# Windowed attention with sink tokens, then a highway layer: a reordered loop, sinks' scores by the batch, and the last batch's loads in runs

## The chip, the cores and the metric

One core of a Trainium2 chip runs the kernel. The metric is the device time of one execution in microseconds; the time of a kernel is the median of its runs. Five engines have queues of their own and work in the order in which their instructions were issued: TensorE (PE, with its weight loads listed as PEld), VectorE (DVE), ScalarE (ACT), GpSimd (POOL) and SyncE (SP, here for DMAs alone). They wait for one another through semaphores.

## The reference

Two layers. The first is attention of 4 batches, 8 heads, 768 tokens and 64 dimensions, in which a token sees itself and the 127 before it, and the first 4 tokens (the sinks). The second mixes each of the 3072 tokens' 512 values with a gated function of itself.

```python
keep = is_sink | in_window                      # pos < 4, or 0 <= rel < 128
scores = np.where(keep, scale * q @ k.T, -1e9)
x = softmax(scores) @ v                         # (B, H, S, D) -> (B*S, H*D)
H = np.maximum(x @ w_h, 0.0)
T = 1.0 / (1.0 + np.exp(-(x @ w_t + b_t)))
out = T * H + (1.0 - T) * x                     # = x + T * (H - x)
```

## The kernel before

The tokens are cut into 24 tiles of 128, six to a batch (`NC`), numbered n = 0 to 23; `b, t = divmod(n, NC)`. Each tile goes through these steps:

- `scores(n)`: TensorE multiplies the keys of tile n with the queries of tiles n and n+1, 16 products of 32 rows, four heads' groups on four row groups. The last tile of a batch has only its own queries.
- `expo(n)`: ScalarE takes the exponential of all of it into E.
- `mask(n)`: VectorE multiplies E by a mask of zeros and ones (the window).
- `sink_scores(n)`, `sink_expo(n)`: for t >= 2, whose windows do not reach the sinks, the scores of the sinks' keys (`sk`, 32 columns used, padded to 128) and their exponential into `es`.
- `values(n)`: TensorE multiplies E of tiles n-1 and n with V, 16 products; for t >= 2 two more with the sinks' values `vs` against `es`. V has a column of ones, so the sum of the weights comes out beside the values.
- `norm(n)`: VectorE takes the reciprocal of the sums and multiplies: X.
- `x_transpose(n)`, `x_copy(n)`: TensorE transposes X into PSUM, ScalarE copies it to XT.
- `bias(n)`, `gate(n)`, `tanh(n)`: TensorE adds the bias (a product with a row of ones) and x @ w_t; ScalarE takes tanh of half of it. `gate_on_act(n)` on ScalarE or, for n = 16 to 22, `gate_value(n)` on GpSimd turns that into T = (tanh + 1) / 2.
- `hidden(n)`: TensorE, x @ w_h. `diff(n)`: VectorE, max(H, 0) - X. `gated(n)`: VectorE, times T, the product of the text.
- `finish(n)`: GpSimd adds X, and SP stores the tile.

The order on every engine is the order in which the program issues (`_keep_traced_order`, L19). After a start written out by hand (L466 to L551), a loop runs from s = 2 to 21 (L552 to L599). A pass is named here by n2 = s + 2, the tile whose scores it computes, 4 to 23; it also handles n1 = s + 1 (mask, values, norm), n0 = s (transpose, gate, hidden) and n9 = s - 1 (difference, product, output). In a pass VectorE's order is diff(n9), mask(n1), gated(n9), transposes of loaded data, then the reciprocal and X of n1. TensorE's is sink_scores(n2), x_transpose(n0), scores(n2), bias(n0), half of gate(n0), values(n1), the other half, hidden(n0). ScalarE's is sink_expo, x_copy, expo, tanh, T. After the loop comes an end written out by hand (L601 to L638).

Queries and keys come from memory with a cast to 16 bits through GpSimd's queue (`load_part`, `load_whole`), 32 partitions at a time, and VectorE transposes them in blocks of 32 (`transpose_qk`, L129; `transpose_tile`, L137). Of batches 0 to 2 a partition gets runs of 8 or 12 neighbouring tokens, and the transposes write with that step; `nat` holds them. Of batch 3 (`whole`) a partition gets single tokens, 32 apart, and the transposes, one for each of six tiles from pass 16 to 21, write neighbouring words. The table `pieces` says in which pass the transposes are, the table `loads` in which pass, and on which side of the output, the loads are issued. `sink_keys(b)` and `sink_values(b)` make `sk` and `vs` by masks. A matmul's result lies in one of the PSUM tiles ps_s (scores), ps_v (values, and in its second half the transposed X), ps_z (gate, and the sinks' scores before it) and ps_h (hidden).

Of the kernel before, what the change touches and what calls it, by code (L numbers as in the profile page):

```python
# [10 lines left out]
FP16 = mybir.dt.float16  # L11
# [21 lines left out]
def kernel(  # L33
# [27 lines left out]
    G = 4  # L61
# [45 lines left out]
    def load_part(b, i, g, which, into=None, engine=pool):  # L107

        t0, nt = segments[b][which][i]
        into = nat[b][which][i] if into is None else into  # L110
        engine.dma_start(  # L111
            out=into[32 * g:32 * g + 32].rearrange("p hg m d -> p hg (m d)"),
            in_=(q, k)[which][b, :, t0:t0 + nt, :].rearrange(
                "(g hg) (r m) d -> g r hg (m d)", g=G, m=nt // 32)[g])

    def load_whole(g, which):
        pool.dma_start(
            out=whole[32 * g:32 * g + 32, which].rearrange("p hg m d -> p (hg m) d"),
            in_=(q, k)[which][B - 1].rearrange(
                "(g hg) (m r) d -> g r (hg m) d", g=G, r=32)[g])  # L120

    def part_loads(b, i, which):

        return [lambda g=g: load_part(b, i, g, which) for g in range(G)]
# [12 lines left out]
    def transpose_tile(n):  # L137

        b, t = divmod(n, NC)
        dst = tr[b].bitcast(FP32).rearrange("p w hg t e -> p (w hg) (t e)")  # L140
        src = whole.bitcast(FP32).rearrange("p w hg m d -> p (w hg) (m d)")
        dve.transpose(out=dst[:, :, t * P:(t + 1) * P], in_=src[:, :, t * P:(t + 1) * P])
# [6 lines left out]
    def load_v_heads(b, h0, h1):  # L149
        pool.dma_start(  # L150
            out=vt[b][0][:, h0:h1].rearrange("p h t e -> p (h t) e")[:, :, 0:D],
            in_=v[b, h0:h1].rearrange("h (t p) d -> p (h t) d", p=P))
# [8 lines left out]
    wt = const.tile([P, KC, DM], FP16, tag="wt")  # L161
    brow = const.tile([P, DM], FP16, tag="brow")
    b32 = const.tile([1, DM], FP32, tag="b32")
    ones = const.tile([P, P], FP16, tag="ones")
    zeros = const.tile([P, H * (D + 1)], FP16, tag="zeros")
    vs32 = const.tile([H * NSINK, B, D + 1], FP32, tag="vs32")
    vmask = const.tile([H * NSINK, H], FP32, tag="vmask")
    skmask = const.tile([P, HG, H], FP16, tag="skmask")
    vs = [const.tile([P, H, D + 1], FP16, tag=f"vs{b}", name=f"vs{b}") for b in range(B)]

    sk = [const.tile([P, HG, 2, P], FP16, tag=f"sk{b}", name=f"sk{b}") for b in range(B)]
# [8 lines left out]
    sp.dma_start(out=b32, in_=moe_b_t.unsqueeze(0))  # L180
    for b in range(B):
        sp.dma_start(out=vs32[:, b, 0:D],
                     in_=v[b, :, 0:NSINK, :])
# [14 lines left out]
    dve.memset(brow, 0.0)  # L198
    dve.memset(skmask, 0.0)
    for g in range(G):  # L200
        for hg in range(HG):
            h = HG * g + hg
            dve.memset(skmask[32 * g:32 * g + 32, hg, h:h + 1], 1.0)
    for tile_v in [tile_v for of_batch in vt for tile_v in of_batch]:
        dve.memset(tile_v[:, :, :, D:D + 1], 1.0)
    dve.memset(vs32[:, :, D:D + 1], 1.0)
    for i in range(2):
        dve.memset(es[i], 0.0)
    dve.memset(sk[0].rearrange("p hg e x -> p (hg e x)"), 0.0)
    dve.memset(vs[0].rearrange("p h e -> p (h e)"), 0.0)  # L210
    for b in range(1, B):
        act.copy(out=vs[b].rearrange("p h e -> p (h e)"), in_=zeros)
        act.copy(out=sk[b].rearrange("p hg e x -> p (hg e x)"), in_=zeros[:, 0:HG * 2 * P])
# [7 lines left out]
    pool.memset(vmask, 1.0)  # L221
    pool.affine_select(out=vmask, in_=vmask, compare_op=ALU.is_ge, fill=0.0, base=0,
                       pattern=[[-NSINK, H]], channel_multiplier=1)
    pool.affine_select(out=vmask, in_=vmask, compare_op=ALU.is_ge, fill=0.0,
                       base=NSINK - 1, pattern=[[NSINK, H]], channel_multiplier=-1)


    def sink_keys(b, engine=pool):
        for hg in range(HG):
            engine.tensor_tensor(  # L230
                out=sk[b][:, hg, :, 0:H * NSINK].rearrange("p e (h s) -> p e h s", s=NSINK),
# [5 lines left out]
    def sink_values(b):  # L237
        pool.tensor_tensor(
            out=vs[b][0:H * NSINK],
            in0=vs32[:, b].unsqueeze(1).to_broadcast([H * NSINK, H, D + 1]),  # L240
            in1=vmask.unsqueeze(2).to_broadcast([H * NSINK, H, D + 1]), op=ALU.mult)
# [12 lines left out]


    def sink_bank(n):
        return (ps_h if n == 3 else ps_z)[:, 0:P]

    def sink_scores(n):
        b, t = divmod(n, NC)  # L260
        first = True
        for hg in range(HG):
            for e in range(2):
                last = hg == HG - 1 and e == 1
                pe.matmul(sink_bank(n),
                          lhsT=sk[b][:, hg, e],
                          rhs=tr[b][:, 0, hg, t * P:(t + 1) * P, e], start=first, stop=last)
                first = False

    def sink_expo(n):  # L270
        nrow = H * NSINK
        act.activation(out=es[n % 2][0:nrow], in_=sink_bank(n)[0:nrow],
                       func=AF.Exp, bias=ebias[0:nrow], scale=SCALE)
# [24 lines left out]

    def values(n):
        b, t = divmod(n, NC)  # L300
        both = av_of(n)
        for i in range(2):
            if t >= 2:
                pe.matmul(both[:, i], lhsT=es[n % 2],
                          rhs=vs[b][:, HB * i:HB * i + HB, :].rearrange("p h e -> p (h e)"),
                          start=True, stop=False, skip_group_check=True)
# [14 lines left out]
    def norm(n):  # L321
# [3 lines left out]
        dve.reciprocal(out=rec, in_=av[:, :, :, D])  # L325
# [348 lines left out]
```

## Time and profile before

| | |
|---|---|
| median of 3 runs | 120.01 us (119.53 to 120.34) |
| the profiled execution | 119.51 us, its span 117.5 us |
| granted clock of TensorE, mean | 0.987 |
| TensorE's first instruction after the loop (bias of tile 22) | starts at 106.70 us |
| DMA | 17.52 MB in 46,160 packets, 38,594 of them under 512 B |

The span is what the profile shows, from the first instruction to the last; the profiled execution took 2.0 us more than that. A line of a group gives the program line, engine, operation, the tiles and shapes, the count, the busy time and the mean in ns, and the idle time before it with its releaser. A line in order of time starts with the start and the duration in us; a bracket shows an idle stretch before it. A window's line has its bounds, its length, then the busy time of PE, PEld, DVE, ACT and POOL with the number of instructions, TensorE's clock, the share of the DMA engines and GB/s.

### The profile page before, as it was taken

The page shows a single profiled execution, that of the slowest core. Times are in us where ns is not written, and L with a number is a line of the kernel's source. Part 1 is how long each engine was busy: PE and PEld are TensorE (multiplying, and loading weights), DVE is VectorE, ACT ScalarE, POOL GpSimd, SP SyncE. Part 2 cuts the span into 40 slices and gives each one's busy share as a digit, 9 for nine tenths or more (in the row PEclk, how much of TensorE's full clock was granted, in tenths as well). Part 3 has the DMA queues.
Part 4 walks back from the last instruction along what each step waited for, and adds up shares of the span by engine and source line. Part 5 has one row for each costly group of instructions (what it writes and reads, how often), then busy time and mean ns, then how long its engine had stood idle before and what let it go on. Part 6 is the DMA issues. An engine that isn't in the chain of part 4 may idle for free.

```text
span 117.5 us, 3064 instructions
## 1 busy us (share of the span) xinstructions
PE 101.4 (86%) x1189; PEld 55.8 (48%) x1189; DVE 97.1 (83%) x186; ACT 91.0 (77%) x116; POOL 85.7 (73%) x118
## 2 busy tenths in 40 slices
PE   5997868599969869799999898999998999999920
PEld 1333445345535435556554454655464556555610
DVE  5589875669995899999998999698889998797580
ACT  0985789659769969899699999798788987964510
POOL 6979997499998997798979999530674336415660
PEclk9999999999999999999999999999999999999995
DMA  3999999989999999999999999999310222022032
GB/s 102 238 204 149 140 144 199 147 116 154 106 153 153 284 280 249 182 169 187 206 213 150 198 164 200 154 196 207 108 72 17 89 95 86 3 95 89 27 150 91
DMA packets 46160, 17.52 MB, mean 149 GB/s; under 512 B 38594, under 2 KB 42434, under 8 KB 46147
## 3 DMA queue, kind: packets, MB, share of 16 engines
q0 software_dynamic: 41744, 9.97, 96.9%
q1 hardware_dynamic: 3938, 6.72, 16.8%
q10 hardware_dynamic: 464, 0.66, 2.2%
q8 instruction: 9, 0.15, 0.5%
q14 instruction: 5, 0.03, 0.1%
HBM read 21.01 MB, written 6.29 MB: 232 GB/s over the span
## 4 chain that ended last, share of the span: by engine, by line
PE 38%; DMA 22%; DVE 21%; issue 8%; POOL 4%; ACT 3%; ACTq 1%; DVEq 0%
PE ps_z L365 10%; DMA wh<-in_moe_w_h_dram 9%; PE ps_h L398 9%; DMA nat<-in_k_dram 5%; DVE DD L402 5%; DMA first<-in_q_dram 5%; DVE E L289 5%; DVE tr L134 4%; PE ps_v L316 4%; PE ps_s L250 3%; DVE X L326 3%; DMA nat<-in_q_dram 3%; PE ps_v L313 2%; DVE DD L406 2%; PE ps_v L353 2%
## 5 line engine op out<-in xcount | busy, mean ns | idle before, releaser
L281 ACT ACTIVATE E<-ps_s,ebias 128x2048 f16<-128x2048 f32 (+1 forms) x24 | 43.7, 1822 | 2.1 <-PE ps_s L250 2.1
L411 POOL TENSOR_TENSOR O<-DD,X 128x512 f32<-128x512 f16 (+1 forms) x24 | 27.1, 1134 | 21.4 <-DVE DD L406 13.1
L365 PE MATMUL ps_z<-wt,XT 128*128 128x512 f16 (+1 forms) x96 | 27.6, 375 | 0.4
L398 PE MATMUL ps_h<-wh,XT 128*128 128x512 f16 (+1 forms) x96 | 24.2, 374 | 1.4 <-DMA wh<-in_moe_w_h_dram 1.4
L289 DVE TENSOR_TENSOR E<-E,mask_std 128x2048 f16<-128x2048 f16 (+1 forms) x20 | 22.8, 1138 | 0.3 <-ACT E L281 0.2
L134 DVE STREAM_TRANSPOSE tr<-nat 128x512 f32<-128x512 f32 (+1 forms) x22 | 19.0, 909 | 2.1 <-DMA nat<-in_q_dram 1.1
L402 DVE SCALAR_TENSOR_TENSOR DD<-ps_h,X 128x512 f16<-128x512 f32 (+1 forms) x24 | 16.2, 677 | 4.3 <-PE ps_h L398 3.5
L382 ACT ACTIVATE TH<-ps_z 128x512 f16<-128x512 f32 (+1 forms) x24 | 14.1, 586 | 5.3 <-PE ps_z L365 4.9
L358 ACT COPY XT<-ps_v 128x512 f16<-128x512 f16 x23 | 13.1, 571 | 5.5 <-PE ps_v L353 5.4
L316 PE MATMUL ps_v<-v,E 128*128 128x65 f16 x184 | 15.4, 195 | 1.8 <-DVE E L289 1.5
L326 DVE TENSOR_TENSOR X<-ps_v,rec 128x512 f16<-128x512 f32 x23 | 15.9, 692 | 0.9
L250 PE MATMUL ps_s<-tr 32*128 32x256 f16 (+1 forms) x384 | 14.3, 264 | 1.5 <-DVE mask L492 0.9
L398 PEld LDWEIGHTS <-XT 128*128 128x128 f16 x100 | 9.7, 98 | 11.8 <-issue 1.5
L316 PEld LDWEIGHTS <-E 128*128 128x128 f16 x192 | 12.2, 97 | 6.4 <-DVE E L289 5.1
L313 PE MATMUL ps_v<-v,E 128*128 128x65 f16 x152 | 15.0, 193 | 0.1
L111 POOL DMA_DIRECT2D nat<-in_k_dram x24 | 13.4, 571 | 0.6 <-DMA nat<-in_k_dram 0.6
L313 PEld LDWEIGHTS <-E 128*128 128x128 f16 x160 | 12.5, 98 | 2.3 <-issue 0.2
L111 POOL DMA_DIRECT2D nat<-in_q_dram x20 | 11.2, 564 | 2.2 <-DMA wh<-in_moe_w_h_dram 1.5
L353 PE MATMUL ps_v<-ident,X 128*128 128x128 f16 x92 | 9.0, 220 | 4.2 <-DVE X L326 4.0
L388 ACT ACTIVATE TH<-TH,half 128x512 f16<-128x512 f16 (+1 forms) x17 | 12.0, 709 | 0.5
L191 PE MATMUL ps_h<-zeros 128*128 128x512 f16 x36 | 10.4, 444 | 1.3 <-DVE zeros L194 1.3
L406 DVE TENSOR_TENSOR DD<-DD,TH 128x512 f16<-128x512 f16 (+1 forms) x24 | 10.4, 433 | 0.5 <-POOL TH L393 0.3
(75 smaller groups left out, 131.2 us busy)
## 6 DMA issues: line engine op xcount, KB each, us to landing
out_dram<-O SPq DMA_DIRECT2D x23, 256.0 KB, 5.1
nat<-in_q_dram POOLq DMA_DIRECT2D x16, 96.0 KB, 6.6
nat<-in_k_dram POOLq DMA_DIRECT2D x16, 96.0 KB, 5.5
v<-in_v_dram POOLq DMA_DIRECT2D x4, 384.0 KB, 9.4
v<-in_v_dram POOLq DMA_DIRECT2D x6, 128.0 KB, 5.3
v<-in_v_dram POOLq DMA_DIRECT2D x1, 768.0 KB, 10.8
whole<-in_q_dram POOLq DMA_DIRECT2D x4, 192.0 KB, 6.4
whole<-in_k_dram POOLq DMA_DIRECT2D x4, 192.0 KB, 7.8
```

What stands on the lines that cost most here:

```text
L111: engine.dma_start(out=into[32 * g:32 * g + 32].rearrange("p hg m d -> p hg (m d)"), in_=(q, k)[which][b, :, t0:t0 + nt, :].rearrange("(g ...
L134: dve.transpose(out=dst[:, :, lo:hi, :], in_=nat[b][which][i].bitcast(FP32)[:, :, lo:hi, :])
L250: pe.matmul(ps_s[:, g, hg, 0:nq * P], lhsT=tr[b][rows, 1, hg, c * P:(c + 1) * P, e], rhs=tr[b][rows, 0, hg, c * P:(c + nq) * P, e], start= ...
L281: act.activation(out=E[n][:, :, :, 0:nq * P], in_=ps_s[:, :, :, 0:nq * P], func=AF.Exp, bias=ebias, scale=SCALE)
L289: return dve.tensor_tensor(out=e3, in0=e3, in1=m[:, 0:nq * P].unsqueeze(1).to_broadcast([P, H, nq * P]), op=ALU.mult)
L313: pe.matmul(slot, lhsT=E[n - 1][:, g, hg, P:2 * P], rhs=v_of(n - 1)[:, h, :], start=first, stop=False, skip_group_check=True)
L316: pe.matmul(slot, lhsT=E[n][:, g, hg, 0:P], rhs=v_of(n)[:, h, :], start=first, stop=True, skip_group_check=True)
L326: dve.tensor_tensor(out=X[n], in0=av[:, :, :, 0:D], in1=rec.unsqueeze(3).to_broadcast([P, 2, HB, D]), op=ALU.mult)
L365: pe.matmul(z_of(n, cols), lhsT=XT[n][:, kc * P:(kc + 1) * P], rhs=wt[:, kc, cols], start=False, stop=(kc == KC - 1))
L398: pe.matmul(h_of(n, cols), lhsT=XT[n][:, kc * P:(kc + 1) * P], rhs=wh[:, kc, cols], start=(kc == 0), stop=(kc == KC - 1))
L402: dve.scalar_tensor_tensor(out=DD[n][:, cols], in0=h_of(n, cols), scalar=0.0, in1=flat(X[n])[:, cols], op0=ALU.max, op1=ALU.subtract)
L411: ins = pool.tensor_tensor(out=O[n][:, cols], in0=DD[n][:, cols], in1=flat(X[n])[:, cols], op=ALU.add)
```

## The change

1. In the passes n2 > 4, VectorE's order becomes mask(n1), diff(n9), reciprocal(n1), gated(n9), X(n1), and then the transposes of loaded data. `norm` gets an argument `between` for what is issued between the reciprocal and X. The values and half of the gate are issued ahead of the loads and outputs in the program.
2. T is computed by ScalarE for all tiles but 22, and in a later place: after x_copy of the next pass, ahead of the exponential.
3. The sinks' scores of a batch are computed at once for its four tiles t = 2 to 5, in pass t = 2 (batch 0: at the start): 16 products with 32 columns each, tile i's into partitions 32i to 32i+31 of ps_z, and one exponential over 128 partitions. `values_of_sinks(n)` then takes the tile's 32 rows of `es` and `vs`, and is issued right after the bias.
4. The bias is a product of one row on a row group of its own, another than that of the sinks' values beside it. For that the bias, the sinks' values (`vs32`) and the masks lie four times, on partitions 32i; SP loads them with 4 and 16 DMAs (1 and 4 before), after VectorE has zeroed them. Six copies of zeros on ScalarE and some zeroing on VectorE go.
5. The last batch's loads take runs of two tokens (`a=2`), and six transposes, each of two tiles of queries or of keys, stand in passes 15 to 20; they write every second word.
6. Loads: V of tiles 4 and 5 go from pass 3 into the start's list; in passes 9 to 15 some loads are issued ahead of the output, the first of a pass behind the mask.

```diff
-    def load_whole(g, which):
-        pool.dma_start(
-            out=whole[32 * g:32 * g + 32, which].rearrange("p hg m d -> p (hg m) d"),
+    def load_whole(g, which, after=None):
+        behind(pool.dma_start(
+            out=whole[32 * g:32 * g + 32, which].rearrange("p hg (m a) d -> p (hg m) (a d)",
+                                                           a=2),
             in_=(q, k)[which][B - 1].rearrange(
-                "(g hg) (m r) d -> g r (hg m) d", g=G, r=32)[g])
+                "(g hg) (m r a) d -> g r (hg m) (a d)", g=G, r=32, a=2)[g]), after)
...
+    def transpose_tiles(which, t0, t1):
+        dst = tr[B - 1].bitcast(FP32).rearrange("p w hg t e -> p w hg (t e)")[:, which]
+        src = whole.bitcast(FP32)[:, which]
+        dve.transpose(
+            out=dst[:, :, t0 * P:t1 * P].rearrange("p hg (m r a) -> p hg m a r", r=32, a=2),
+            in_=src[:, :, 4 * t0:4 * t1].rearrange("p hg (m a) d -> p hg m a d", a=2))
...
+    dve.memset(b32, 0.0)
+    for i in range(G):
+        sp.dma_start(out=b32[32 * i:32 * i + 1, :], in_=moe_b_t.unsqueeze(0))
...
-    for b in range(1, B):
-        act.copy(out=vs[b].rearrange("p h e -> p (h e)"), in_=zeros)
-        act.copy(out=sk[b].rearrange("p hg e x -> p (hg e x)"), in_=zeros[:, 0:HG * 2 * P])
+    dve.memset(sk.rearrange("p b hg e x -> p (b hg e x)"), 0.0)
+    for b in range(B):
+        for i in range(G):
+            sp.dma_start(out=vs32[32 * i:32 * i + H * NSINK, b, 0:D],
+                         in_=v[b, :, 0:NSINK, :])
...
-                pe.matmul(sink_bank(n),
-                          lhsT=sk[b][:, hg, e],
-                          rhs=tr[b][:, 0, hg, t * P:(t + 1) * P, e], start=first, stop=last)
+                for i in range(G):
+                    t = 2 + i
+                    pe.matmul(ps_z[32 * i:32 * i + 32, 0:P], lhsT=sk[:, b, hg, e],
+                              rhs=tr[b][:, 0, hg, t * P:(t + 1) * P, e],
+                              start=first, stop=(hg == HG - 1 and e == 1))
...
+    def values_of_sinks(n):
+        b, t = divmod(n, NC)
+        if t >= 2:
+            rows = slice(32 * (t - 2), 32 * (t - 1))
+            for i in range(2):
+                pe.matmul(av_of(n)[:, i], lhsT=es[b % 2][rows],
+                          rhs=vs[b][rows, HB * i:HB * i + HB, :].rearrange("p h e -> p (h e)"),
+                          start=True, stop=False, skip_group_check=True)
...
-    def norm(n):
+    def norm(n, between=None):
         dve.reciprocal(out=rec, in_=av[:, :, :, D])
+        other = between() if between is not None else None
         dve.tensor_tensor(out=X[n], in0=av[:, :, :, 0:D],
...
-    def bias(n, cols=ALL):
-        pe.matmul(z_of(n, cols), lhsT=ones, rhs=brow[:, cols], start=True, stop=False)
+    def bias(n, cols=ALL, group=None):
+        lhsT, rhs = (ones, brow) if group is None else (
+            ones_g[32 * group:32 * group + 1], brow[32 * group:32 * group + 1])
+        pe.matmul(z_of(n, cols), lhsT=lhsT, rhs=rhs[:, cols], start=True, stop=False)
...
-        return n < 16 or n == N - 1
+        return n != N - 2
...
-    tiles = {n: [n + 2] for n in range(RUNS * NC - 2, N - 2)}
+    tiles.update({15: [(0, 0, 2)], 16: [(0, 2, 4)], 17: [(1, 0, 2)], 18: [(0, 4, 6)],
+                  19: [(1, 2, 4)], 20: [(1, 4, 6)]})
...
+    second.insert(4, lambda: load_v(4))
+    second.append(lambda: load_v(5))
...
         if n2 > 4:
-            if n2 % NC >= 2:
-                sink_scores(n2)
-                sink_expo(n2)
+            if n2 % NC == 2:
+                sinks(n2 // NC)
             x_transpose(n0)
             x_copy(n0)
+            gate_on_act(n9)
             scores(n2)
-        bias(n0)
-        if n2 > 4:
+            bias(n0, group=(n1 % NC + 1) % G)
+            values_of_sinks(n1)
             expo(n2)
+        else:
+            bias(n0)
         gate_value(n9)
+        masked = mask(n1) if n2 > 4 else None
         diff(n9)
...
         else:
-            mask(n1)
-        last = gated(n9)
-        for load in loads[n2][0]:
-            load()
+            outputs(n0)
+            gate(n0, parts=range(0, 2))
+            values(n1)
+            last = norm(n1, between=lambda: gated(n9))
+        for i, load in enumerate(loads[n2][0]):
+            load(after=masked if i == 0 else None)
...
-        if n2 > 4:
-            outputs(n0)
-            gate(n0, parts=range(0, 2))
-            values(n1)
-            norm(n1)
         gate(n0, parts=range(2, KC))
-        tanh(n0)
+        tanh(n0, gate_too=False)
         hidden(n0)
```

## The prediction

> **What bounds the kernel now.** I read the page first (busy shares, slices, chain), then the windows of 4 us, then VectorE's instructions in order of time. The page and the chain:
>
> ```profile
> span 117.5 us, 3064 instructions
> ...
> PE 101.4 (86%) x1189; PEld 55.8 (48%) x1189; DVE 97.1 (83%) x186; ACT 91.0 (77%) x116; POOL 85.7 (73%) x118
> ...
> PE 38%; DMA 22%; DVE 21%; issue 8%; POOL 4%; ACT 3%; ACTq 1%; DVEq 0%
> ```
>
> No engine is the bound alone: TensorE and VectorE hand the chain to each other. Up to 26.6 us the chain is nearly all transfers (wh lands at 22.4, the queries of batch 1 at 26.56). The windows (VectorE is the third figure after the length, TensorE the first) show who is short of time later:
>
> ```profile
> 50.00:54.00 4.00, 4.00 (x56) 2.30 (x53) 3.83 (x7) 3.97 (x6) 3.59 (x5) 1.00 1.86 187
> ...
> 90.00:94.00 4.00, 3.89 (x51) 2.27 (x50) 3.91 (x8) 3.44 (x5) 2.15 (x3) 1.00 0.17 66
> 98.00:102.00 4.00, 4.00 (x53) 2.34 (x51) 3.09 (x6) 3.31 (x4) 1.81 (x3) 1.00 0.17 66
> ```
>
> In the middle VectorE is 96% busy; at the end it has 0.9 of 4 us free and TensorE none. The clock is 1.00 throughout, so no price below changes with it. One pass (n2 = 21) of VectorE in order of time, start, duration:
>
> ```profile
> 94.96 0.69 DVE L402 SCALAR_TENSOR_TENSOR DD<-ps_h,X 128x512 f16<-128x512 f32 x1 [0.26 <-PE ps_h L398]
> 95.57 1.22 DVE L289 TENSOR_TENSOR E<-E,mask_std 128x2048 f16<-128x2048 f16 x1
> 96.70 0.42 DVE L406 TENSOR_TENSOR DD<-DD,TH 128x512 f16<-128x512 f16 x1
> 97.04 0.70 DVE L142 STREAM_TRANSPOSE tr<-whole 128x512 f32<-128x512 f32 x1
> 97.70 0.21 DVE L325 RECIPROCAL rec<-ps_v 128x8 f32<-128x8 f32 x1
> 97.94 0.69 DVE L326 TENSOR_TENSOR X<-ps_v,rec 128x512 f16<-128x512 f32 x1
> ```
>
> The difference waits 0.26 for hidden; the mask stands behind it; TensorE's values wait for the mask. That is a ring: hidden, difference, mask, values, second half of the gate, hidden. The next difference is at 98.92, so a pass is 3.96 us. Starts lie closer than durations say (neighbours overlap by 0.08), so I count from start to start: difference 0.61, mask 1.13, product 0.34, transpose 0.63 here and 0.94 for a run of 8, X 0.61.
>
> **Order of VectorE.** With the mask first the ring is cut: the mask needs only an exponential of the pass before. In its place comes a ring on VectorE with one visit to TensorE: mask 1.22; then values, 0.06 to start (mask end 73.51, values 73.57), 15 steps of 0.03, 0.19 for the last and 0.08 to the reciprocal: 0.78; the difference (0.53 left after overlap) runs beside it, so 0.25 stays idle; reciprocal 0.13, product 0.34, X 0.61, transpose. Without the transpose 3.08; with a run of 8 4.02; with a 0.63 one 3.71. The transposes now stand behind X, so they cover x_transpose, scores and gate of the next pass.
>
> A second ring goes through TensorE: x_transpose 0.32, scores 0.57, bias and sinks' values 0.32, half gate 0.43, values 0.52, 0.27 to the reciprocal, then 0.13 + 0.34 + 0.69 + 0.05: 3.64. ScalarE: XT 0.48, T 0.63, exponential 1.92, tanh 0.63: 3.66. So no late pass is under about 3.67, or under 3.71 where a tile's transpose is.
>
> **Sinks at once.** 64 products stay 64, but 16 exponentials (0.35, 0.25 effective) become 4: ScalarE wins 12 x 0.25 = 3 us, off the path. TensorE's 16 scores of four products take 0.23 each. A batch's 16 narrow ones cost 0.23 if four column groups run together, 16 x 0.055 = 0.9 if not; I take 0.25, being nearest to scores (16 products of 256 columns on four row groups in 0.57, where one of 260 columns alone takes 0.11 from start to start). They need queries of four tiles: x_transpose in pass 8 stands behind the transposes of 1,1.
>
> **Row groups.** Bias 0.22 and two sinks' values of 0.11 (0.22) are 0.44 in line, 0.22 together; I take 0.32, both ends in the range (6 late passes x 0.12 = 0.7 each way). The Trainium skill, "TensorEngine Tiling (Array Packing)", Key Properties, says that changing the tiling mode drains TensorE. No row here prices it; bias and sinks' values follow scores, which are in 32-row form already, so by that rule only the four batches' narrow scores add changes.
>
> **T on ScalarE.** Six tiles' 0.62 leave GpSimd, which has over 1.8 us free per pass there, and add 0.63 to ScalarE, which reaches 3.66 of 3.71: no cost while the pass is not shorter. T moves behind XT and ahead of the exponential; the product comes 1 us after it. If that cover goes, 0.63 a pass.
>
> **Last batch.** The eight loads move runs of two tokens, half as many packets. GpSimd's issue is 0.93 for 1,536 pieces and 0.91 for a load of V with 1,024, 0.57 for one with 64: about 0.8, 1 us saved in all, hidden. The first load of a pass now waits for the mask; behind it on GpSimd stand the output and later loads, and the output waits for the product anyway. It keeps them off the masks, which took 1.30 and 1.70 at 67.80 and 71.81 where issues of whole and v ran, against 1.22: 0.5 us. The transposes now write every second word. The groups by shape:
>
> ```profile
> L134 DVE STREAM_TRANSPOSE tr<-nat 128x512 f32<-128x512 f32 x14 | 15.0, 1080 | 2.1 <-DMA nat<-in_q_dram 1.1 <-DMA nat<-in_k_dram 0.8 <-ACT nat L489 0.2
> L142 DVE STREAM_TRANSPOSE tr<-whole 128x512 f32<-128x512 f32 x6 | 4.2, 705 | 0.0
> ```
>
> L134 writes 8 or 12 words apart, L142 adjacent ones. Two apart is nearer to adjacent: 0.70; the other end is 1.08, 6 x 0.31 = 1.9 us more. The Trainium skill, "SBUF — State Buffer", Specifications (cachelines), says that two accesses in a 16-byte line keep full bandwidth: by that rule also 0.70; the two rows above agree with it, but no row has this step.
>
> **Start.** SP issues 20 small transfers for 5, at 0.29 to 0.75 each (its b and vs rows): done by 12 to 18 us, sinks' values read them on GpSimd at 15.6 to 20.1, batch 1's loads queued behind. ScalarE loses six copies of 0.61 in a stretch where it then waits for queries anyway, but its bias copy (8.26) now waits for four transfers; behind it is the first exponential at 10.22, with 1.34 idle before. VectorE's zeroing changes by under 0.5, against 0.98 idle at 5.28. TensorE's 1.44 wait for wh covers a late start up to that; no cover beyond. V of tiles 4 and 5 goes ahead in GpSimd's queue: batch 1's keys 0.9 later, not before needed. I take 0.
>
> **The sum,** X end to X end. Passes 5 to 9: scores(6) needs all of batch 1's first transposes, as before (34.6). X(6) ends at 41.1, not 43.0, since nothing stands in front. But the outputs on GpSimd wait for the product, and the loads of 1,1 stand behind them: outputs 2 and 3 start at 37.3, not 35.88, so the keys land near 46.6, not 45.18; their transposes end at 48.05 and scores(9) waits: X(8) ends at 51.3, before 51.4. So -0.1.
> Passes 10 to 15: 4.02 + 4.02 + 3.57 (half mask) + 3.76 (first tile of a batch, half the values) + 4.11 + 4.17 (scores(15) waits for a transpose) = 23.65, before 51.39 to 75.73, 24.34: -0.7.
> Passes 16 to 22: 3.71 + 3.71 + 3.67 + 3.45 + 3.71 + 3.71 + 3.67 = 25.63, before 75.73 to 102.60, 26.87: -1.2.
> Pass 23: mask(23) leaves the way to X(22): 3.5 for 4.03, -0.5; the rest as before.
> Together -2.5. The profiled execution took 119.51 (span 117.5 and 2.0 around it), so 117.0; the median was 0.5 above it: **117.5**.
>
> **The rivals.**
> *The waiting moves into the reciprocal (slower).* If gate(n0) ends after the mask, values start late and the idle 0.25 grows on the engine that is 96% busy. In pass n2 = 16 on, x_transpose starts 0.58 before the mask and gate ends 0.32 + 0.57 + 0.32 + 0.43 = 1.64 later, at 1.06, mask end at 1.22: a margin of 0.16, and of none in passes without a transpose. From 0.14 a pass (2.5 over 18) it eats all; idle 0.5, as half of the longest waits of the reciprocal now (4.0 us in four), makes 18 x 0.25 = 4.5: 122.0. Against: 15 of 18 passes have a transpose. Chance 0.14.
> *The new step of the transposes costs as L134:* +1.9, 119.4. For it: nothing shows a step of two; against: above. Chance 0.18.
> *The loads are not late:* the 1.9 us that X(6) wins last to the end, 115.6. For: the transposes' waits on transfers sum to only 1.9 us now; against: GpSimd is busy 36.5 of 40 us from 34 to 74. Chance 0.18.
> *Forecast,* 116.0 to 118.8: 0.50.
>
> **How the numbers follow.** About 1% is what a measurement of this kernel can tell: faster is under 118.8, slower over 121.2. Faster: 0.47 of the forecast, 0.18, and 0.03 of the stepped transposes: 0.68. Slower: 0.12 of the reciprocal's case and 0.01: 0.13. Same: 0.19. The range leaves out half of each end case: 114.9 (115.6 with the row groups' 0.7) to 120.8.
>
> **What would show it.** The difference right behind the mask without a wait; the reciprocal with 0.2 to 0.3 idle in front; x_transpose under 0.1 behind X; whole's transposes at 0.70; passes 16 to 22 at 3.7; four es exponentials. Wrong if the reciprocal waits over 0.4 in most passes, if masks start late for the exponential (ScalarE the bound), or if VectorE waits over 1 us for the keys of 1,1.

## The result, and the profile after

The changed kernel took 126.56 us (median of 4 runs, 125.30 to 128.94), the kernel before 119.77 us beside it (median of 4, 118.63 to 120.34): a ratio of 1.054, 95% interval 1.042 to 1.067. It is slower by 5.4%, where the prediction had 2% faster and a range that ended at 120.8. A ratio here and below is taken over the undisturbed runs alone, those within 1.5% of the fastest of their kernel, so it can differ from the ratio of the medians.

The profiled execution took 126.72 us, its span 125.0 us: 7.5 more than before. The page of the changed kernel (span, granted clock over 40 slices of 3.1 us, shares of the chain):

```profile
span 125.0 us, 3076 instructions
...
PE 104.0 (83%) x1189; PEld 51.3 (41%) x1189; DVE 100.9 (81%) x189; ACT 87.3 (70%) x104; POOL 83.7 (67%) x112
...
PEclk9999995999999985599999999999999999999985
...
PE 43%; DVE 33%; ACT 9%; issue 8%; POOL 3%; DVEq 1%; POOLq 0%
```

VectorE has 3.8 us more of work, and its share of the chain has grown from 21 to 33%. The clock, which the prediction held constant, falls to a half in two places, near 20 and near 50 us. The windows of the changed kernel (bounds, length, busy time of PE, PEld, DVE, ACT, POOL, clock, DMA share, GB/s):

```profile
46.00:50.00 4.00, 3.94 (x50) 2.07 (x51) 0.45 (x1) 3.07 (x4) 4.00 (x7) 0.50 0.65 133
50.00:54.00 4.00, 4.00 (x38) 1.94 (x36) 3.39 (x6) 1.69 (x4) 2.51 (x4) 0.65 0.82 156
...
98.00:102.00 4.00, 3.82 (x61) 2.08 (x60) 3.10 (x7) 3.48 (x6) 0.76 (x2) 1.00 0.19 70
```

Between 46 and 50 us VectorE works 0.45 of 4 us, while GpSimd works all of it and TensorE runs at half clock. Later both TensorE and VectorE have some slack and neither is the bound by its busy time.

Where the time went shows in the start times of X, the last step of a tile's attention:

| from | to | before | predicted | after | difference to before |
|---|---|---|---|---|---|
| start of the span | X(6) | 42.32 | 40.4 | 42.69 | +0.4 |
| X(6) | X(8) | 8.38 | 10.2 | 13.18 | +4.8 |
| X(8) | X(14) | 24.34 | 23.65 | 25.88 | +1.5 |
| X(14) | X(21) | 26.87 | 25.63 | 27.09 | +0.2 |
| X(21) | X(22) | 4.03 | 3.5 | 3.78 | -0.3 |
| X(22) | end of the span | 11.56 | 11.56 | 12.38 | +0.8 |

Two thirds of the loss lie in two passes. Of the last row, nothing is lost in the computation (from X(23) to ScalarE's last DMA 6.4 us in both); the 0.8 stand behind it, until the last outputs have landed.

**One late pass.** VectorE in the changed kernel in order of time (start, duration), the pass that answers to the one shown of before:

```profile
102.52 1.23 DVE L303 TENSOR_TENSOR E<-E,mask_std 128x2048 f16<-128x2048 f16 x1
103.67 0.68 DVE L426 SCALAR_TENSOR_TENSOR DD<-ps_h,X 128x512 f16<-128x512 f32 x1
104.62 0.21 DVE L344 RECIPROCAL rec<-ps_v 128x8 f32<-128x8 f32 x1 [0.27 <-PE ps_v L335]
104.75 0.40 DVE L430 TENSOR_TENSOR DD<-DD,TH 128x512 f16<-128x512 f16 x1
105.06 0.68 DVE L347 TENSOR_TENSOR X<-ps_v,rec 128x512 f16<-128x512 f32 x1
105.67 1.85 DVE L303 TENSOR_TENSOR E<-E,mask_std 128x2048 f16<-128x2048 f16 x1
```

The first five lines are the predicted pass: the difference right behind the mask without a wait, 0.27 idle before the reciprocal (0.25 predicted). The sixth is not: a mask of 1.85 for 1.22. The groups by shape of the changed kernel say that this one is no exception:

```profile
L303 DVE TENSOR_TENSOR E<-E,mask_std 128x2048 f16<-128x2048 f16 x16 | 23.6, 1477 | 0.0
...
L303 DVE TENSOR_TENSOR E<-E,mask 128x2048 f16<-128x2048 f16 x4 | 5.5, 1377 | 0.5 <-ACT E L295 0.5
...
L151 DVE STREAM_TRANSPOSE tr<-whole 128x512 f32<-128x512 f32 x6 | 4.2, 703 | 0.0
L303 DVE TENSOR_TENSOR E<-E,mask_std 128x1024 f16<-128x1024 f16 x4 | 4.2, 1052 | 0.0
```

The three groups of masks sum to 33.3 us; before they were 20.0 + 4.9 + 2.7 = 27.6. So 5.7 us of VectorE's time are gone on masks of the same size. Beside the slow mask at 105.67 GpSimd's part of the trace has:

```profile
101.51 1.16 POOL L435 TENSOR_TENSOR O<-DD,X 128x512 f32<-128x512 f16 x1 [3.24 <-DVE DD L430]
105.28 1.16 POOL L435 TENSOR_TENSOR O<-DD,X 128x512 f32<-128x512 f16 x1 [2.61 <-DVE DD L430]
```

The output that starts at 105.28 ends at 106.44; the mask ends at 107.52, 1.08 later, as if it had begun only then. The output at 101.51 ended at 102.67, only 0.15 after its mask began (102.52), and that mask took 1.23: it too ended 1.08 after the output. The same holds for every long mask of full size after the start: outputs end at 40.40, 57.79, 74.84, 79.41, 83.47, 106.44 and 110.21, and the masks beside them 1.07 to 1.11 later. One half mask took 2.17 and ended 0.56 after an output. It also holds for the two slow masks of the kernel before: its outputs ended at 68.01 and 72.42, its masks at 69.10 and 73.51. The second pair, VectorE and then GpSimd, in the kernel before:

```profile
71.81 1.70 DVE L289 TENSOR_TENSOR E<-E,mask_std 128x2048 f16<-128x2048 f16 x1
```

```profile
71.25 1.17 POOL L411 TENSOR_TENSOR O<-DD,X 128x512 f32<-128x512 f16 x1
```

The Trainium skill, "SBUF — State Buffer", section "Who interferes with whom", says that a VectorE instruction with two inputs in SBUF contends with a GpSimd instruction that reads SBUF, and calls the port pair that they share an exclusive lock. The trace agrees, and the lock lasts for the whole output here: 1.07 to 1.11 us are left of a full mask after the output's end, whenever the mask began. The other steps of a pass on VectorE have at most one input in SBUF, and none of them was lengthened in any run: differences took at most 0.69 us, X 0.69, reciprocals 0.21, the transposes of `whole` 0.71.

Before, the output ran in the stretch after the product: transposes, reciprocal, X, difference, some 2.3 us in which VectorE reads at most one input from SBUF beside PSUM. In the new order only X and the transposes are between the product and the next mask: 0.61 + 0.63 or 0.94 us, and 0.61 alone in passes without transposes, for an output of 1.15.

**Pass 8.** It works the other way too: an output that comes second waits for the mask. GpSimd of the changed kernel, and then of the kernel before, in the same stretch:

```profile
39.24 3.24 POOL L435 TENSOR_TENSOR O<-DD,X 128x512 f32<-128x512 f16 x2 [1.21 <-DVE DD L430]
42.43 1.09 POOL L119 DMA_DIRECT2D nat<-in_k_dram  x2
43.51 1.06 POOL L119 DMA_DIRECT2D nat<-in_q_dram  x2
44.58 1.68 POOL L246 TENSOR_TENSOR sk<-tr,skmask 128x64 f16<-128x64 f16 x2
```

```profile
35.88 2.26 POOL L411 TENSOR_TENSOR O<-DD,X 128x512 f32<-128x512 f16 x2 [0.34 <-DVE DD L406]
38.09 1.20 POOL L111 DMA_DIRECT2D nat<-in_k_dram  x2
39.28 1.06 POOL L111 DMA_DIRECT2D nat<-in_q_dram  x2
40.35 0.55 POOL L230 TENSOR_TENSOR sk<-tr,skmask 128x64 f16<-128x64 f16 x2
```

Outputs 2 and 3 start 3.4 us later, since the product stands behind the reciprocal now, and take 3.24 for 2.26; four loads follow; then the keys of the sinks of batch 1 (`sink_keys`), held to 1.68 for 0.55 by the mask at 44.65. They are done over 5 us later than before. In the new kernel all sinks' scores of a batch are asked for in pass 8, and stand in front of TensorE's whole pass:

```profile
46.05 0.67 PE L277 MATMUL ps_z<-tr,sk 128*32 128x128 f16 x16 [2.81 <-POOL sk L246]
```

TensorE stands for 2.81 us, and works at half clock when it starts again. The windows of 1 us:

```profile
43.00:44.00 1.00, 0.24 (x2) 0.00 (x0) 1.00 (x2) 0.80 (x2) 1.00 (x2) 1.00 0.67 225
...
46.00:47.00 1.00, 0.94 (x20) 0.63 (x20) 0.45 (x1) 0.23 (x1) 1.00 (x2) 0.50 0.83 137
...
52.00:53.00 1.00, 1.00 (x6) 0.46 (x5) 1.00 (x2) 0.00 (x0) 0.94 (x2) 0.59 0.55 95
53.00:54.00 1.00, 1.00 (x23) 0.58 (x21) 1.00 (x2) 0.73 (x2) 0.83 (x1) 1.00 0.73 246
```

### The profile page after: what moved, and what is told of

It reads as the page before. It is cut to its first block, busy times and chain, and to the rows that moved or that the text cites. A ratio compares the mean times of both kernels' runs of the same rounds, so it can differ in the third digit from the quotient of the medians.

```text
span 125.0 us, 3076 instructions
## 1 busy us (share of the span) xinstructions
PE 104.0 (83%) x1189; PEld 51.3 (41%) x1189; DVE 100.9 (81%) x189; ACT 87.3 (70%) x104; POOL 83.7 (67%) x112
## 4 chain that ended last, share of the span: by engine, by line
PE 43%; DVE 33%; ACT 9%; issue 8%; POOL 3%; DVEq 1%; POOLq 0%
PE ps_z L389 10%; DVE E L303 10%; PE ps_h L422 8%; DVE X L347 6%; DVE tr L144 6%; PE ps_s L265 6%; ACT E L295 5%; PE ps_v L335 5%; PE ps_v L375 4%; PE ps_v L332 4%; DVE DD L430 3%; ACT XT L380 2%; PE ps_z L385 2%; PE ps_v L318 2%; DVE DD L426 2%
## 5 line engine op out<-in xcount | busy, mean ns | idle before, releaser
L435 POOL TENSOR_TENSOR O<-DD,X 128x512 f32<-128x512 f16 (+1 forms) x24 | 28.2, 1176 | 27.3 <-DVE DD L430 16.9
L389 PE MATMUL ps_z<-wt,XT 128*128 128x512 f16 (+1 forms) x96 | 29.1, 393 | 0.0
L303 DVE TENSOR_TENSOR E<-E,mask_std 128x2048 f16<-128x2048 f16 (+1 forms) x20 | 27.8, 1392 | 0.0
L422 PE MATMUL ps_h<-wh,XT 128*128 128x512 f16 (+1 forms) x96 | 25.0, 385 | 0.0
L265 PE MATMUL ps_s<-tr 32*128 32x256 f16 (+1 forms) x384 | 15.3, 275 | 4.6 <-DVE tr L144 3.3
L344 DVE RECIPROCAL rec<-ps_v 128x8 f32<-128x8 f32 x23 | 4.7, 206 | 15.4 <-PE ps_v L335 14.6
L335 PE MATMUL ps_v<-v,E 128*128 128x65 f16 x184 | 14.1, 197 | 2.9 <-DVE E L303 2.6
L412 ACT ACTIVATE TH<-TH,half 128x512 f16<-128x512 f16 (+1 forms) x23 | 16.4, 714 | 0.1
L335 PEld LDWEIGHTS <-E 128*128 128x128 f16 x192 | 12.1, 99 | 8.1 <-DVE E L303 6.7
L332 PE MATMUL ps_v<-v,E 128*128 128x65 f16 x152 | 13.1, 196 | 0.1
L332 PEld LDWEIGHTS <-E 128*128 128x128 f16 x160 | 11.6, 100 | 2.9 <-issue 1.1
L265 PEld LDWEIGHTS <-tr 32*128 32x128 f16 x384 | 7.8, 95 | 9.4 <-DVE tr L144 5.0
```

The lines of the kernel that those rows point to most:

```text
L265: pe.matmul(ps_s[:, g, hg, 0:nq * P], lhsT=tr[b][rows, 1, hg, c * P:(c + 1) * P, e], rhs=tr[b][rows, 0, hg, c * P:(c + nq) * P, e], start= ...
L303: return dve.tensor_tensor(out=e3, in0=e3, in1=m[:, 0:nq * P].unsqueeze(1).to_broadcast([P, H, nq * P]), op=ALU.mult)
L332: pe.matmul(slot, lhsT=E[n - 1][:, g, hg, P:2 * P], rhs=v_of(n - 1)[:, h, :], start=first, stop=False, skip_group_check=True)
L335: pe.matmul(slot, lhsT=E[n][:, g, hg, 0:P], rhs=v_of(n)[:, h, :], start=first, stop=True, skip_group_check=True)
L389: pe.matmul(z_of(n, cols), lhsT=XT[n][:, kc * P:(kc + 1) * P], rhs=wt[:, kc, cols], start=False, stop=(kc == KC - 1))
L422: pe.matmul(h_of(n, cols), lhsT=XT[n][:, kc * P:(kc + 1) * P], rhs=wh[:, kc, cols], start=(kc == 0), stop=(kc == KC - 1))
```

## The experiments

The theory from these traces: the new order of VectorE costs the time, through GpSimd. It pushes the output onto a mask, and GpSimd's queue so late that the sinks' keys stop TensorE. The rivals: the narrow sinks and the row groups cost time on TensorE by themselves; the new places of loads and small transfers do; T on ScalarE does.

**The order alone, put into the kernel before.**

```diff
+        if n2 > 4:
+            mask(n1)
         diff(n9)
+        outputs(n0)
+        gate(n0, parts=range(0, 2))
+        values(n1)
...
-            mask(n1)
-        last = gated(n9)
...
+            last = norm(n1, between=lambda: gated(n9))
...
-        if n2 > 4:
-            outputs(n0)
...
-            norm(n1)
```

> The kernel before with VectorE's new order alone (mask, difference, reciprocal, product, X, transposes); all else as before. Theory C: slower than before by 3 us or more, 123 to 127, with masks of 1.5 to 1.9 beside outputs. Rival (the order is harmless, the other parts cost): 118 to 121.

Measured: 125.62 us (124.27 to 128.13) beside 119.44, ratio 1.041 (1.028 to 1.054). Nothing of the other parts is in this kernel, and pass 8 is there again. TensorE, and then GpSimd, in its trace:

```profile
44.49 0.65 PE L265 MATMUL ps_z<-tr,sk 128*128 128x128 f16 x4 [2.82 <-POOL sk L230]
```

```profile
37.67 3.24 POOL L413 TENSOR_TENSOR O<-DD,X 128x512 f32<-128x512 f16 x2 [1.40 <-DVE DD L408]
...
43.03 1.67 POOL L230 TENSOR_TENSOR sk<-tr,skmask 128x64 f16<-128x64 f16 x2
```

The output 3.24, the sinks' keys 1.67, TensorE's wait 2.82 and the clock 0.50 from 44 to 50 us are those of the changed kernel. So neither the narrow sinks nor the loads' places are needed for that stall.

**The order undone in the changed kernel** (the same edit the other way; the sinks, row groups, loads and T stay new).

> The changed kernel with VectorE's order of before (difference, mask, product, transposes, reciprocal, X); sinks by the batch, row groups, T on ScalarE, the start and the last batch's loads stay changed. Theory C (the loss comes from the new order: the product, and with it the output on GpSimd, lands where the next mask or product on VectorE is held up, and GpSimd's queue runs late): 118.5 to 121, masks near 1.22 from pass 6 on. Rival (sinks by the batch, row groups or the start cost it): 124 or more.

Measured: 123.36 us (121.68 to 125.32), ratio 1.023 (1.009 to 1.037): 3.2 us less than with the new order, and 2.3% still lost. The order is the larger part, not all. The order alone cost 4.1%, all but the order 2.3%, the whole 5.4%.

**The sinks' keys ahead of the pass's loads and outputs.**

```diff
+        if n2 >= NC and n2 % NC == 0:
+            sink_keys(n2 // NC)
         for i, load in enumerate(loads[n2][0]):
...
-        if n2 >= NC and n2 % NC == 0:
-            sink_keys(n2 // NC)
```

> The changed kernel with one move on GpSimd: sink_keys(b) goes ahead of the pass's loads and outputs. Theory A (pass 8: TensorE waits 2.8 us in sinks(1) for sink_keys(1), which stands on GpSimd behind outputs and loads; after that idle stretch its granted clock is 0.50 to 52.6 us): the wait goes, the clock stays 1.00 from 43 to 54 us, the time falls by 4 to 5 us to about 122. Rival B (the new order of VectorE is too long a ring in itself): at most 1 us, 125.5 or more, with the loss in other passes.

Measured: 124.79 us (122.96 to 125.98), ratio 1.032 (1.017 to 1.047). The stall in pass 8 is gone: from X(6) to X(7) 5.27 us for 8.36, the clock 1.00 from 38 to 50 us. The gain, some 2 us, is half of what was expected. In the traces 3.1 us were won in this pass, but X(6) had come 1.1 later (43.82 for 42.69), in an execution in which the clock was 0.50 from 10.8 to 14.2 and from 21.1 to 24.5; behind the pass the lead stays between 1.7 and 2.0 us to X(22). The masks that an output meets are still there (1.84 in pass 9, 1.85 in passes 21 and 22).

**The outputs one pass later, behind the next mask.**

```diff
-    finished = {4: (), 5: (0, 1), 6: (2, 3), N - 1: ()}
+    finished = {4: (), 5: (0, 1)}
...
-        for n in finished.get(n2, (n9,)):
-            finish(n, after=last if n2 < 7 else None)
+        for n in finished.get(n2, (n9 - 1,)):
+            finish(n, after=masked)
```

> The changed kernel with the outputs on GpSimd one pass later, each behind the next pass's mask (from pass 6 on one output per pass). Theory A2 (an output on GpSimd holds up the mask on VectorE, each slow mask ends 1.1 us after the output beside it): full masks 1.22 to 1.27 instead of 1.48 in the mean; since GpSimd reaches sink_keys(1) near 41 us, the wait of pass 8 goes too: 118.5 to 120.5. Rival (the masks are slow for another reason, such as ScalarE or transfers): masks stay near 1.48 and the time falls only by what pass 8 gives, to 122.

Measured: 130.89 us (130.01 to 131.19), ratio 1.090 (1.081 to 1.098): slower by 4 us, against the expectation. The masks did become short (one of 1.45 is left in the passes). VectorE and then GpSimd show what became long:

```profile
56.07 1.20 DVE L303 TENSOR_TENSOR E<-E,mask_std 128x2048 f16<-128x2048 f16 x1
57.20 0.66 DVE L426 SCALAR_TENSOR_TENSOR DD<-ps_h,X 128x512 f16<-128x512 f32 x1
58.08 0.21 DVE L344 RECIPROCAL rec<-ps_v 128x8 f32<-128x8 f32 x1 [0.21 <-PE ps_v L335]
58.20 1.89 DVE L430 TENSOR_TENSOR DD<-DD,TH 128x512 f16<-128x512 f16 x1
```

```profile
58.64 1.16 POOL L435 TENSOR_TENSOR O<-DD,X 128x512 f32<-128x512 f16 x1
```

The product reads two inputs from SBUF as the mask does, and now it is the one that meets the output: its mean is 706 ns over the 23, for 416 in the changed kernel. It stands on the way to X, the mask's delay partly beside it; so this exclusion is dearer. The miss supports the mechanism, and the gaps say that no free place for the output (1.15) is left in many passes of this order: the difference (0.66) and the reciprocal (0.21) leave under 1 us between mask and product, and from the end of the product to the start of the next mask it was mostly 0.51 to 1.45 us in the changed kernel.

**Both edits together.**

> Both moves. Theory A and A2 together: 118 to 120, no more than 0.5 us below the second kernel alone if that already takes the wait of pass 8 away. Rival B: over 122, with a reciprocal that waits over 0.4 us in most passes.

Measured: 129.42 us (128.82 to 130.08), ratio 1.079 (1.069 to 1.089): the keys win 1.5 us here too, and the products stay long (721 ns).

**TensorE kept busy while it waits**: 14 products of zeros ahead of the sinks' scores of pass 8.

```diff
+            if n2 == 8:
+                for i in range(14):
+                    pe.matmul(ps_z, lhsT=zeros[:, 0:P], rhs=zeros[:, 0:DM], start=True, stop=True)
             if n2 % NC == 2:
                 sinks(n2 // NC)
```

> The changed kernel with 14 products of zeros into ps_z ahead of sinks(1) in pass 8, so that TensorE is busy while it waits; nothing else moves. If the clock falls because TensorE stood idle, it stays 1.00 from 46 to 53 us, the wait itself remains, and the time falls by about 2.5 us (X(7) comes 5.0 us after the wait's end now, 3.1 after a wait at full clock in pass 20): 124. If the clock has another cause, it falls all the same: 126.5.

Measured: 126.96 us (125.50 to 128.17), ratio 1.054: no gain. In the trace the clock stays 1.00 from 42 to 52 us, and from the sinks' scores to X(7) it takes 3.1 us (46.78 to 49.90) for 5.0 (46.05 to 51.05): half clock costs 1.9 us there. But the zeros ended at 46.78, and in this run the keys were ready at 43.8 already: the products themselves were the wait. The price of the clock is shown, a saving is not.

**The start mended.** In the changed kernel the sinks' values of batch 0 (`sink_values`, 1.13 us on GpSimd at 15.05) run beside mask(1), which takes 2.62; TensorE idles, and the clock is 0.50 from 19 to 22 us. Here GpSimd's `sink_values` and batch 1's loads stand behind mask(1), once with the keys early and once with the old order:

```diff
-    sink_values(0)
...
-    mask(1)
+    mask_1 = mask(1)
...
+    sink_values(0, after=mask_1)
...
```

> The changed kernel with sink_keys early and, at the start, sinks' values and batch 1's loads issued behind mask(1) on GpSimd. If sinks' values of batch 0 hold up mask(1) (1.85 to 2.62 in four of five profiles, 1.22 in the other) and TensorE's clock falls after the idle stretch that follows, mask(1) takes 1.22, the clock stays 1.00 from 18 to 26 us, X(2) starts near 22.0 instead of 24 to 25; a gain of about 2 us over sink_keys alone, 122.5, and runs that lie closer together. If the loads behind it on GpSimd matter more, X(4) comes no earlier and the time stays near 124.5.

Measured: 123.14 us (122.30 to 124.74), ratio 1.035 (1.023 to 1.048).

> VectorE's order of before with all other parts of the change, and the start's sinks' values behind mask(1). Theory C with the start's race: 0 to 2 us below the old order alone, 117.5 to 120; it can beat the kernel before only by what sinks by the batch and the last batch's transposes give, at most 2 us. Rival: no difference to the old order alone.

Measured: 122.34 us (121.13 to 123.73), ratio 1.021 (1.009 to 1.032). In both traces mask(1) takes 1.22 and the early clock stays up (X(2) at 21.7 and 22.2 us, 23.83 in the changed kernel), but the ratios are those of the same kernels without the edit (1.032 and 1.023). By time the start's price is too small to tell. In the run with the zeros, where the start was not mended, mask(1) took 1.22 by itself: the collision comes and goes. Nor is the collision all that lowers the clock: the run without the wait for the mask (below) has the same mended start, a mask(1) of 1.22 and the same waits of TensorE, 0.35 and 1.10, and its clock was 0.50 from 18.4 to 21.9 all the same (X(2) at 23.43).

The second of these two traces shows the rest of the loss: with the old order and a clean start it keeps step with the kernel before up to X(10) (58.64 for 58.78) and then loses 3 us to X(13), 73.56 for 70.49.

**The loads back in their old places** (old order and mended start as in the last run).

```diff
-    put(v_halves(2), ((8, 1, 1), (9, 0, 1)))
-    put(segment_loads(2, 1), ((8, 1, 1), (9, 1, 2), (10, 0, 2), (10, 1, 3)))
+    put(v_halves(2), ((8, 1, 1), (9, 1, 1)))
+    put(segment_loads(2, 1), ((8, 1, 1), (9, 1, 2), (10, 1, 5)))
...
-        ((11, 0, 2), (11, 1, 1), (12, 0, 2), (12, 1, 1), (13, 0, 2)))
-    put(v_halves(3), ((14, 0, 1), (15, 0, 1)))
+        ((11, 1, 3), (12, 1, 3), (13, 1, 2)))
+    put(v_halves(3), ((13, 1, 1), (14, 1, 1)))
```

> The old order of VectorE with the start mended, and now also the loads in the places they had before (both V halves, the second half of batch 2 and the whole last batch behind the pass's outputs, the last V halves one pass earlier, no wait for the mask in front of any). The narrow sinks, the row groups, T on ScalarE and the two-token runs of the last batch stay. Theory A (the second part of the loss lies in the loads' new places ahead of outputs on GpSimd): X(10) to X(13) in about 11.8 us as before, not the 14.9 of the old order with new loads, and the end by about 2.4 us earlier: 118 to 120. Rival B (the loss in passes 11 to 13 comes from the narrow sinks or the row groups on TensorE, or T on ScalarE): time stays at 121.5 to 123 and X(10) to X(13) at over 13.5 us.

Measured: 120.21 us (120.02 to 120.94) beside 120.54 (118.00 to 121.48), ratio 1.017 (1.009 to 1.026). From X(10) to X(13) it takes 12.2 us, in the kernel with the new places 14.9, before 11.7. By the ratios, 1.017 for 1.021, the gain cannot be told.

**The new places, without the wait for the mask** (`load()` for `load(after=masked if i == 0 else None)`).

> The old order with the start mended, loads in their new places, but the first load of a pass no longer waits for the mask. If the wait is what holds GpSimd (4.07 us idle in front of the first whole load in the run with it): that idle is gone, X(10) to X(13) under 13 us, time 118.5 to 120.5. If it is the place (an issue ahead of the outputs, held until a ring of the queue or an earlier transfer is free): the same idle of 3 to 4 us stands there, and the time stays within 1 us of the run with the wait (122.3).

Measured: 122.41 us (120.31 to 123.46), ratio 1.020 (0.999 to 1.040), X(10) to X(13) again 14.9: in the traces the place costs, not the wait. The median is 2.2 us above that of the old places (122.41 for 120.21), but the ratios, 1.020 and 1.017, do not tell the two apart. GpSimd in front of the first load of the last batch, with new places and no wait, and then with old places:

```profile
50.23 1.44 POOL L161 DMA_DIRECT2D v<-in_v_dram  x1
...
62.37 1.43 POOL L125 DMA_DIRECT2D whole<-in_q_dram  x2 [3.94 <-DMA v<-in_v_dram]
```

```profile
51.08 1.46 POOL L161 DMA_DIRECT2D v<-in_v_dram  x1
...
60.21 2.17 POOL L125 DMA_DIRECT2D whole<-in_q_dram  x3 [1.21 <-DMA v<-in_v_dram]
```

The load waits for the landing of a half of V that was issued eight DMAs earlier on the same queue. It lands 10.7 us after the end of its issue with the new places and 7.7 with the old ones: with the new places the two halves were issued 2.0 us apart (48.25 and 50.23), with the old ones 3.6 (47.51 and 51.08), an output between them. That their closeness is what makes the landing late wasn't tried by itself. The output of the pass stands behind the waiting load, and the outputs after it came so late that two products met them (1.29 and 1.30).

**The new order on the old places** (with the keys early and the start mended).

> The changed kernel with sinks' keys ahead of the pass's loads and outputs, the start mended, and the loads in the places they had before (behind the outputs, no wait for the mask): the new order of VectorE on the old queue of GpSimd. Theory A (two losses that add up: the loads' places cost some 2 us with either order, and the masks held up by outputs remain, since the window after the product is 0.61 to 1.24 us against an output of 1.15): 123.1 less about 2, so 120.5 to 122, with three to six masks still over 1.5 us, among them the two of passes 21 and 22, which have no transposes behind X. Rival B (the loads ahead of the outputs were what pushed outputs onto masks): only the masks of passes 21 and 22 stay slow, and the time is 117.5 to 119.5, under the kernel before. Rival C (order alone): 123 to 125, unchanged.

Measured: 122.47 us (121.38 to 123.88) beside 119.82, ratio 1.021 (1.013 to 1.030); 0.7 us under the same kernel with the new places. The time lies just beyond the first theory's upper end, and far from the second's 117.5 to 119.5: masks of 1.80, 1.83, 2.03, 1.85 and 1.85 and a product of 1.10 remain, and GpSimd waited 2.73 and 2.07 for halves of V in the old places too. What the places are worth with this order stays open: the medians differ by 0.7 us, the ratios are 1.035 and 1.021, and their intervals overlap.

**T of tiles 16 to 21 back on GpSimd** (old order, old places).

> The old order, the mended start and the old loads, and T of tiles 16 to 21 back on GpSimd. If T on ScalarE costs nothing, as predicted, the time is that of the old loads alone within 0.7 us. If ScalarE is the bound of the late passes (0.63 more in each of six), up to 2 us less; if GpSimd is, 1 us more.

Measured: 121.08 us (119.71 to 121.91), ratio 1.020 (1.005 to 1.034), 0.9 above the kernel with T on ScalarE, inside the scatter: T on ScalarE costs nothing and gives nothing here that can be told.

None of these kernels beats the kernel before. The best has the old order, the mended start, the old places of the loads and all else new, and takes 120.21 us; whether it is level with the kernel before (median 120.54 beside it) or slower (ratio 1.017) stays open. In its profiled execution X(22) starts at 105.90, against 105.94 before: up to there the two are level. What its span is longer by, 0.8 us, lies behind X(22), and not by the order: from X(22) to the end of the span it is 11.6 us before and with the order alone, and 12.3 to 12.6 in the changed kernel and every variant of it. Which part of the change does that was not tried.

## Why the prediction was wrong

**The step that failed is "Order of VectorE", where it cuts the ring.** The ring was priced by VectorE's and TensorE's own durations, with a mask of 1.22 in each pass; who else reads SBUF beside it was not asked. Moving the product behind the reciprocal moved the start of the output, which takes 1.15, from a place with mostly 2.1 to 3.2 us to the next mask to one with mostly 0.51 to 1.45. Shown by the order alone (4.1% slower on the kernel before) and by the moved outputs, which moved the delay from mask to product.

**"Outputs on GpSimd wait for the product" was seen and priced too low.** The prediction had outputs 2 and 3 start at 37.3 and followed GpSimd's queue to the keys of 1,1. Measured are a start at 39.24 and 3.24 us for the two. And on the same queue it passed over `sink_keys`, which feeds the sinks' scores of pass 8: the row 40.35 of before stood right behind those loads. For "Sinks at once" only the transposes of 1,1 were named as what the scores wait for. That is the 2.81 us.

**"The clock is 1.00 throughout, so no price below changes with it"** held for a kernel whose TensorE never stood that long. A new wait of 2.81 us cost 1.9 us more by the clock.

**"It keeps them off the masks, 0.5 us" was a misreading of before's profile.** The 1.30 and 1.70 were put down to issues of loads; the outputs that ended at 68.01 and 72.42 fit both to 1.09 us. Read rightly, those two rows showed the effect that the new order ran into. And loads ahead of the output did not win 0.5: with the old order X(10) to X(13) took 2.7 us longer with them in the traces, where a load that waited for a landing held the output behind it.

**"Start. I take 0."** X(2) came 2.5 us later and X(6) 0.4 later, where 1.9 earlier was predicted: the order's gain up to there went in the collision of `sink_values(0)` with mask(1) and in mask(6) at 1.80. With the start mended X(6) came at 41.08 and 41.22 in the two kernels with the new order. That the start's part reaches the end isn't shown.

**Late passes: 3.67 to 3.71 predicted, 3.77 to 3.81 in four of seven** (in the last of these a mask of 1.85 stands where the others have a transpose). The ring through TensorE and the 0.25 idle were right. The sum of 25.63 missed by 1.46: a mask of 1.59 (4.07), and 4.39 in the pass of batch 3's sinks, where the 16 products (0.34; 0.25 taken) stand ahead of x_transpose and, writing ps_z, wait 0.56 for the tanh that reads it. That second wait was not in the prediction.

**Right:** the transposes of the last batch at 0.703 (0.70); four exponentials for 16; bias and sinks' values side by side in 0.32 where XT is ready (37.12 to 37.44), though in other passes the sinks' values wait for the copy of XT, whose transposed X lies in their PSUM tile (the copy ends at 83.51, they start at 83.56, and from bias to gate it is 0.59); T on ScalarE at no cost that can be told; no sign of the rival in which the reciprocal waits in each pass: 0.20 to 0.30 in ten of the eighteen passes from pass 6 on, none in three. The slower rival was a different mechanism from the one that came.

## What to carry to other kernels

Before reordering an engine, list what the neighbours run in the stretch that each moved step opens or closes: an addition on GpSimd and a two-input step on VectorE that meet cost the whole overlap, so the add needs a window as long as itself among VectorE steps with at most one input in SBUF. When a step is moved, follow every consumer on the queue behind it to the next engine that waits, down to small ones like the sinks' keys here. A row that stands out in the profile of before (a mask of 1.70 among masks of 1.22) should be explained to the tenth of a microsecond by an end time of another engine before it is put down to anything.

## What the runs showed of the hardware

TensorE's clock was 0.50 from 46.0 us, at its first work after a wait of 2.81 us, and came back only at 52.8. At the start it fell at 18.7, with no wait over 1.27 us, in a stretch from 16 to 20 us in which TensorE was busy 1.63 of 4, and was back at 22.1. The Trainium skill, "TensorE: Matmul & The Clock Gate", section "What's actually happening", gives one idle window of about 3.4 us for the fall and one busy one for the return, and says that the window is free-running. The traces agree with the window: these four changes of the clock lie 1, 7 and 2 times 3.41 us apart. They do not agree that a window must be idle: in the 3.41 us before the falls TensorE was busy 0.67 us (46.0), 1.32 (18.7), and up to 2.02 (at 44.9 in the run with the mended start and early keys). And the return took one such window at 18.7, but two at 46.0, with TensorE busy 3.35 of 3.41 in the first. In four traces with the mended start TensorE stood the same 0.35 and 1.10 us at the start, and the clock fell in one of them; that it depends on where the waits lie against the window fits this, and was not tried by itself.

An issue on GpSimd's queue waited for the landing of the transfer eight issues before it. The longest of these waits were for a half of V: 0.72 in the kernel before, 1.21, 3.94, 1.70, 2.73 and 2.07 in the runs above; earlier in the span others were for weights and keys (1.50 for `wh` and 0.55 for keys in the kernel before). What holds the issue, the queue or the program's own semaphores, no run tells.
